# First input chunk loaded by column halves, first weights loaded whole, and one set of down forms moved by three units, in a one-core gated attention and MLP kernel

## The chip, the core and the metric

The kernel runs on one core of a Trainium2 chip. The core has a matrix engine (PE), a vector engine (DVE), a scalar engine (ACT), GpSimd (POOL) and a queue engine (SP); each takes its own instructions strictly in order and waits on semaphores for the others. PE writes to eight PSUM banks of 128 partitions x 2 KB, from which DVE or ACT copy results to SBUF. DMAs are issued from the queues of SP, ACT and POOL and all run on the same 16 DMA engines. The metric is device time in microseconds (us), the median of several executions; lower is better.

## What is computed

```python
def reference(A_x, A_wqkv, A_wo, B_x, B_w_gate, B_w_up, B_w_down, gate_w):
    x = A_x                                           # 1 x 2048 x 1024, bf16
    g = _sigmoid((x * gate_w).sum(-1, keepdims=True))
    a = _A_ref(x, A_wqkv, A_wo)   # 32 heads of 32, each position sees 8 positions, 2 apart
    b = _B_ref(x, B_w_gate, B_w_up, B_w_down)         # gelu(x Wg) * (x Wu), then Wd; 3584 wide
    return g * a + (1 - g) * b
```

## The kernel before

All large products are done with seven instead of eight block products (a Strassen scheme of Winograd's form). A *unit* is one 2x2 block product: 256 output rows of one projection against one half ("super chunk") of 1024 rows of the input. In it PE does seven forms of four matmuls of 128x128 by 128x512 each: `p1` (L11 R11), `p2` (L12 R21), `p5` (S1 T1), `p6` (S2 T2), `p73` (S3 T3 and S4 R22) and `p4` (L22 T4). R11 to R22 are quarters of the transposed input, T1 to T4 differences of them; L11, L12, L22 are quarters of the weights, S1 to S4 sums of them. Sums and differences are made on DVE ahead of their use: `sums_pair` (four `TENSOR_TENSOR` of 128x1024 at L313) for a pair of gate and up weights, and for the first input T1 to T4 by `T` in `head` (L1260). ACT copies most results out of PSUM (L349 to L397); each `p73` ends in one DVE add, L389, which frees two banks that the next units need.

The order on each engine is written out by hand. `head` does the first two weight pairs (four units, `f[0]` to `f[3]`) while the input is still arriving. The input's first two 512-row chunks come as loaded rows (`load_xn`), are transposed on PE in 128x128 blocks (`pe_transpose_chunk`, L217, four blocks into one bank as a *group*) and copied from PSUM by DVE (L223) and ACT (L221) in turn. In `head` the order is: transposes of chunk 0; `p1` of f[0] and f[1]; `patterns` (a small PE transpose L262, then DVE copies L264, L265); `p2` of f[0] and f[1]; f[2] and f[3]'s first forms; transposes of chunk 1; T1; then the weight sums of both pairs (`s0`, `s1`) spread between the other differences; the gate's matmuls (`gate_chunk`, L272); and `p5` of all four, `p6`, `p73`, `p4`. The weights of the two pairs arrive by `load_pair` (L168) in column halves of 128, so that L11 and L12 of both are there first, then the input's second chunk, then the other column halves, which only the sums and `p4` read. All these loads go through SP's queue, except two of the first chunk's four on ACT's.

After `head` a loop runs units 2 to n-1. Between two units' forms DVE runs background tasks, picked by priority and by a credit of planned DVE time per unit (`run_bg`). Among them: products of the local attention (L581, L588), their reduction on PE with `R_` (L593, 24 small matmuls in a row), softmax (L688 to L710), and `t_forms`, which makes differences of the down and output weights for the last stage, in nine sets of two blocks (L869 once, L872 twice, for a set), and stores them to DRAM. Sets 4 and 5 (`N1` and `N1 + 1`) are loaded together at unit `TB` and may be formed from unit `TB + 1` on.

Of the kernel before, what the change touches and what calls it, by code (L numbers as in the profile page):

```python
# [10 lines left out]
BF16 = mybir.dt.bfloat16  # L11
# [4 lines left out]
P = 128  # L16
SC = 512
# [5 lines left out]
NJ = 4  # L23
SJ = AC // NJ
NEG = -1.0e9
NWARM = 6
QG = 4

KB = 512
# [34 lines left out]
def _win_ap(src: bass.AP, dims):  # L64
    return AP(src.tensor, src.offset, [list(src.ap[0])] + [list(d) for d in dims])
# [3 lines left out]
def kernel(  # L69
# [12 lines left out]
    nc = tc.nc  # L82
# [3 lines left out]
    x = A_x.rearrange("b s d -> (b s) d")  # L86
    o2 = out.rearrange("b s d -> (b s) d")
    KT = D // P
    HK = KT // 2
# [13 lines left out]
    def reg(kb, n):  # L103
        o = int(kb * KB)
        return arena[:, o:o + n]

    def reg3(kb, a, b):
        return reg(kb, a * b).rearrange("p (a b) -> p a b", a=a)

    def reg4(kb, a, b, c):  # L110
        return reg(kb, a * b * c).rearrange("p (a b c) -> p a b c", a=a, b=b)

    def regf(kb, n):
        return reg(kb, 2 * n).bitcast(F32)
# [3 lines left out]
    def bank(i):  # L118
        return banks[:, i, :]
# [18 lines left out]
    with tc.manual_schedule(engines={mybir.EngineType.PE, mybir.EngineType.DVE, mybir.EngineType.Activation,  # L138
                                    mybir.EngineType.SP, mybir.EngineType.Pool}):
        xn = [reg3(R_XN + 8 * i, 4, D) for i in range(2)]  # L140

        def load_xn(c):
            for j in range(4):
                (nc.scalar if c == 0 and j % 2 else nc.sync).dma_start(
                    out=xn[c % 2][:, j, :], in_=x[c * SC + j * P:c * SC + (j + 1) * P, :])

        load_xn(0)
        warm = reg(R_ST, SC)
        V.memset(warm, 0.0)
        for i in range(NWARM):  # L150
            pw = bank((2, 4, 6, 0)[i % 4])
# [8 lines left out]
        raw0 = reg4(R_W0, 2, KT, 2 * P)  # L160
        raw1 = reg4(R_W0 + 8, 2, KT, 2 * P)
        sums0, sums1 = (reg(o, 4 * 2 * HK * P).rearrange("p (f m k n) -> p f m k n", f=4, m=2, k=HK)
                        for o in (R_WQK + 48, R_W0 + 16))

        def load_pair(dst, i, a=0, b=2 * P, k0=0, k1=KT):
            c0 = 2 * P * i
            for m, src in ((0, B_w_gate), (1, B_w_up)):
                nc.sync.dma_start(out=dst[:, m, k0:k1, a:b],  # L168
                                  in_=src[k0 * P:k1 * P, c0 + a:c0 + b].rearrange("(k p) n -> p k n", p=P))

        gwr = small.tile([KT, P], BF16, tag="gwr", bufs=1)
        nc.gpsimd.dma_start(out=gwr[:], in_=gate_w.rearrange("(k p) -> k p", p=P))
        load_pair(raw0, 0, 0, P, 0, HK)
        load_pair(raw0, 0, 0, P, HK, KT)
        load_pair(raw1, 1, 0, P)
        load_xn(1)
        load_pair(raw0, 0, P, 2 * P)
        load_pair(raw1, 1, P, 2 * P)

        class XF:  # L180
            pass
# [2 lines left out]
        for s in range(2):  # L184
            b0 = R_X[s]
            f = XF()
# [10 lines left out]
        def flat(a):  # L197
            return a.rearrange("p a b -> p (a b)")
# [8 lines left out]
            f = xf[s]  # L207
            TT(out=flat(f.T3), in0=flat(f.R22), in1=flat(f.R12), op=ALU.subtract)

        def pe_transpose_chunk(c, dst, slots, by_k=False):  # L210
            order = [(j, k0) for j in range(4) for k0 in range(0, KT, 4)]
            if by_k:
                order.sort(key=lambda g: g[1])
            for n_, (j, k0) in enumerate(order):
                p_ = bank(slots[n_ % len(slots)]).bitcast(BF16)[:, 0:SC].rearrange("p (a b) -> p a b", a=4)
                for kk in range(4):
                    nc.tensor.transpose(out=p_[:, kk, :], in_=xn[c % 2][:, j, (k0 + kk) * P:(k0 + kk + 1) * P],  # L217
                                        identity=ident[:])
                d = dst[:, k0:k0 + 4, j * P:(j + 1) * P]
                if n_ % 2 == 1:  # L220
                    nc.scalar.copy(out=d, in_=p_)  # L221
                else:
                    V.tensor_copy(out=d, in_=p_)  # L223
# [34 lines left out]
        def patterns():  # L258
            with nc.allow_low_precision("block pattern of zeros and ones"):
                V.tensor_reduce(out=R_[:], in_=ident[:].rearrange("p (h d) -> p h d", d=4), axis=AX.X, op=ALU.add)  # L260
            pgw = bank(7).bitcast(BF16)[:, 0:KT]
            nc.tensor.transpose(out=pgw, in_=gwr[:], identity=ident[0:KT, 0:KT])  # L262
            gwc = small.tile([P, KT], BF16, tag="gwc", bufs=1)
            V.tensor_copy(out=gwc[:], in_=pgw)  # L264
            V.tensor_copy(out=gwrep, in_=gwc[:].rearrange("p (k o) -> p k o", o=1).to_broadcast([P, KT, GC]))  # L265
# [61 lines left out]
        for c in range(2, 4):  # L327
            dst = (xf[1].c1, xf[1].c2)[c - 2]
# [73 lines left out]
        now = [0]  # L402
# [69 lines left out]
        def at_end(n, fn):  # L472
            post.setdefault(n, []).append(fn)
# [321 lines left out]
        for s in range(2):  # L795
            for t in range(NT):
                n_ = Q0 + NT * s + t
# [44 lines left out]
        N1 = 4  # L842
        TB = Q0 + 2 * NT + 1
        TC = NQKV + 1

        def tf_set(q):
            o = R_TF[q % 3] if q < N1 or q >= N1 + 2 else R_TB[q - N1]
            return [reg3(o + NP * k, NP, SC) for k in range(4)]

        def tf_load(q):  # L850
            i0 = NP * q
            for k, a in enumerate(((0, 0), (0, 1), (1, 0), (1, 1))):
                for sl, src in r_parts(*a, i0, i0 + NP):
                    nc.sync.dma_start(out=tf_set(q)[k][:, sl.start - i0:sl.stop - i0, :], in_=src)

        tf_q = [0]

        def t_forms():
            for q in range(NQ):
                tf_q[0] = q  # L860
                if q in (N1 + 1, N1 + 2):
                    tft.prio = 3.9 if q == N1 + 1 else 4.5
                    tasks.sort(key=lambda t_: t_.prio)
                while q >= N1 and now[0] < (TB if q < N1 + 2 else TC) + 1:
                    yield None
                r11, r12, r21, r22 = tf_set(q)
                n_ = NP * SC
                both = _win_ap(flat(r11), [[n_, 2], [1, n_]])
                TT(out=both, in0=_win_ap(flat(r12), [[2 * n_, 2], [1, n_]]), in1=both, op=ALU.subtract)  # L869
                yield 1.14  # L870
                for o_, a, b_ in ((r22, r22, r11), (r21, r21, r22)):
                    TT(out=flat(o_), in0=flat(a), in1=flat(b_), op=ALU.subtract)  # L872
                    yield 0.61
                for k, t in enumerate((r11, r22, r12, r21)):
                    nc.gpsimd.dma_start(out=t_d[k][:, NP * q:NP * q + NP, :], in_=t)
                if q + 3 < (N1 if q < N1 else NQ if q >= N1 + 2 else 0):
                    tf_load(q + 3)
# [5 lines left out]
        tft = bg(t_forms(), 6, Q0 + 4)  # L883

        def tf_close():
# [3 lines left out]
            tasks.sort(key=lambda t_: t_.prio)  # L889
            load_v()  # L890

        at_end(TFE - 1, tf_close)

        plan = [dict(A11=4, R11=5, A12=2, R21=7, A21=6, A22=3, T1=1, T2=9, S=8, AD=0, L5=4, R5=5, L6=7, R6=1,
                     T3=8, L7=4, R7=5, T4=9, L4=1, R4=7, R22=6),
# [333 lines left out]
        n = len(units)  # L1229
# [19 lines left out]
        def head():  # L1249
            xs, f = xf[0], []  # L1250
            for w, sm, o in ((raw0, sums0, R_ATTN), (raw1, sums1, R_PROD)):
                for m in range(2):
                    u = Unit(gu_forms(w, sm, m), xs, ("gate", "up")[m], None)
                    u.T = reg3(o + 4 * m, 2, SUP)
                    f.append(u)
            units[0:Q0] = f[2:]
            for u, x, v, y, z in zip(f, (3, 5, 1, 7), (1, 7, 3, 5), (0, 2, 4, 6), (1, 3, 5, 7)):
                u.lie(x, v, y, z)
            f[3].fin = lambda: bg(h_task(f[2].T, f[3].T, 1, 0), 0, now[0] + 1)
            T = lambda o_, a, b_: TT(out=flat(o_), in0=flat(a), in1=flat(b_), op=ALU.subtract)  # L1260
            s0, s1 = sums_pair(raw0, sums0), sums_pair(raw1, sums1)

            pe_transpose_chunk(0, xs.c1, (3, 5, 1, 7))
            f[0].p1_()
            f[1].p1_()
            patterns()
            f[0].p2()
            f[1].p2()
            f[2].p1_()
            f[3].p1_()  # L1270
            f[2].p2()
            pe_transpose_chunk(1, xs.c2, (3, 5, 1), True)
            T(xs.T1, xs.R12, xs.R11)
            next(s0)
            next(s1)
            f[3].p2()
            for c in range(2):
                gate_chunk(c, bank(3 + 2 * c))
            next(s0)
            T(xs.T2, xs.R22, xs.T1)  # L1280
            next(s1)
            T(xs.T3, xs.R22, xs.R12)
            for i, u in enumerate(f):
                u.p5(regf(R_XN + 2 * i, SC))
            for g in (s0, s0, s1, s1):
                next(g)
            T(xs.T4, xs.R21, xs.T2)
            for u in f:
                u.p6()
            next(sq0)  # L1290
            next(sq0)
            for u in f[:3]:
                u.p73()
            for g in (sq0, sq0, sq1, sq1):
                next(g)
            for u in f[:3]:
                u.p4()
            bg(h_task(f[0].T, f[1].T, 0, 0), 0, Q0 + 1)
# [59 lines left out]
```

## Time and profile before

| | |
|---|---|
| median of 3 executions | 718.57 us (717.97 to 718.95) |
| the profiled execution | 718.77 us |
| its span, first to last instruction | 717.0 us |
| granted TensorE clock, mean of the core | 1.000 |
| PE idle before matmuls, waiting for L389 on DVE | 2.2 us in 2 waits |
| input and weights: packets of 256 bytes, 14 to 16 us | 217 GB/s |
| input and weights: packets of 2 KB, 19 to 21 us | 388 GB/s |
| a later moment with weight rows of 512 bytes, 296 to 297 us | 352 GB/s |

In the timelines a line gives start, busy time (both in us), engine, source line, operation, what it writes and reads with shapes, and a count; in brackets stands how long the engine had been idle before and what ended that. The chain of waits is followed back from the last instruction to whatever released each step, so what stands in it set the end of the run.

### The profile page before, as it was taken

Reading aid. Unit: us, or ns where it says so; the run is one execution under the profiler, and the core shown is the slowest. Engines: PE = TensorE matmul, PEld = TensorE weight load, DVE = VectorE, ACT = ScalarE, POOL = GpSimd, SP = SyncE. Lnnn points to the kernel's source line nnn. Section 1 sums busy time; section 2 is a strip of 40 time slices with the busy share of each in tenths; the row PEclk is TensorE's granted clock in tenths of the full one; section 3 lists DMA queues with packets and bytes.
Section 4 is the critical chain, followed back from the end, with each engine's and each line's share of the span. In section 5 each row is a group of like instructions: output and inputs, shape, how many; then the busy total and the mean of one; then the engine's idle time right before and its main releaser. Section 6 shows DMA issues by size and latency. Waiting matters only on the chain.

```text
span 717.0 us, 10673 instructions
## 1 busy us (share of the span) xinstructions
PE 705.7 (98%) x4043; PEld 408.4 (57%) x4099; DVE 669.0 (93%) x633; ACT 330.7 (46%) x603; POOL 142.4 (20%) x245
## 2 busy tenths in 40 slices
PE   8999999999999999999999999999999999999998
PEld 5466666655544444444444444444447886758887
DVE  3969989989999999999999999999699899799997
ACT  5554445444466565555555555555322321132431
POOL 1223445323232332121300010101100002100011
PEclk9999999999999999999999999999999999999999
DMA  9975434478285667765762763474950799995951
GB/s 252 274 188 169 151 125 154 155 239 306 92 269 175 214 216 240 223 214 180 234 178 89 279 208 122 161 262 148 426 226 29 300 405 397 417 431 218 403 211 59
DMA packets 94707, 162.03 MB, mean 226 GB/s; under 512 B 23632, under 2 KB 71152, under 8 KB 90304
## 3 DMA queue, kind: packets, MB, share of 16 engines
q1 hardware_dynamic: 77632, 105.46, 42.7%
q0 software_dynamic: 16304, 48.29, 19.9%
q10 hardware_dynamic: 720, 7.60, 2.7%
q8 instruction: 32, 0.52, 0.3%
q14 instruction: 19, 0.16, 0.1%
HBM read 112.17 MB, written 54.14 MB: 232 GB/s over the span
## 4 chain that ended last, share of the span: by engine, by line
PE 91%; DVE 3%; DMA 3%; issue 1%; ACT 0%; DVEq 0%; POOLq 0%; ACTq 0%
PE banks L343 63%; PE banks L1046 19%; PE banks L1079 7%; PE banks L593 2%; DMA arena<-h_d 1%; DMA h_d<-arena 1%; DVE arena L389 1%; DVE arena L753 1%; PE banks L217 1%; DVE arena L747 1%; DMA arena<-in_A_x_dram 0%; DVE arena L313 0%; DVE arena L588 0%; DVE arena L1260 0%; DVE arena L581 0%
## 5 line engine op out<-in xcount | busy, mean ns | idle before, releaser
L343 PE MATMUL banks<-arena 128*128 128x512 bf16 x2191 | 484.1, 379 | 5.4 <-DVE arena L389 2.2
L343 PEld LDWEIGHTS <-arena 128*128 128x128 bf16 x2240 | 245.9, 110 | 242.2 <-issue 8.1
L1046 PE MATMUL banks<-arena 128*128 128x256 bf16 x1260 | 138.5, 273 | 0.0
L1046 PEld LDWEIGHTS <-arena 128*128 128x128 bf16 x1260 | 123.3, 98 | 15.4 <-issue 0.5
L389 DVE TENSOR_TENSOR arena<-banks,arena 128x1024 bf16<-128x1024 f32 x80 | 97.4, 1219 | 11.1 <-PE banks L343 6.5
L370 ACT COPY arena<-banks 128x512 f32<-128x512 f32 x80 | 46.9, 587 | 129.7 <-PE banks L343 129.7
L351 ACT CAST arena<-banks 128x512 bf16<-128x512 f32 x104 | 60.9, 585 | 42.8 <-PE banks L343 42.2
L747 DVE TENSOR_TENSOR arena<-arena 128x4096 bf16<-128x4096 bf16 (+1 forms) x41 | 73.5, 1818 | 0.3
L753 DVE TENSOR_TENSOR arena<-arena 128x2048 bf16<-128x2048 bf16 (+2 forms) x54 | 68.1, 1261 | 0.9
L250 POOL DMA_DIRECT2D h_d<-arena x28 | 20.4, 731 | 222.6 <-DVE arena L244 144.6
L1079 PE MATMUL banks<-arena 128*128 128x512 bf16 x281 | 62.6, 379 | 0.7 <-DMA arena<-h_d 0.4
L378 ACT COPY banks<-banks 128x512 f32<-128x512 f32 x80 | 45.6, 570 | 23.7 <-PE banks L343 20.8
L1004 DVE TENSOR_TENSOR arena<-arena 128x2304 bf16<-128x2304 bf16 x40 | 53.3, 1352 | 0.5
L365 ACT COPY banks<-banks 128x512 f32<-128x512 f32 x80 | 46.1, 576 | 14.2 <-PE banks L343 13.1
L1051 ACT COPY banks<-banks 128x256 f32<-128x256 f32 x60 | 21.4, 356 | 62.2 <-PE banks L1046 62.0
L588 DVE TENSOR_TENSOR arena<-arena 128x4096 bf16<-128x4096 bf16 x21 | 47.9, 2284 | 0.3 <-ACT arena L370 0.2
L1079 PEld LDWEIGHTS <-arena 128*128 128x128 bf16 x288 | 28.1, 98 | 34.2 <-DMA arena<-h_d 0.9
L349 ACT ACTIVATE arena<-banks 128x512 bf16<-128x512 f32 x56 | 33.5, 597 | 20.4 <-PE banks L343 20.4
L927 DVE TENSOR_TENSOR arena<-arena 128x2048 bf16<-128x2048 bf16 (+1 forms) x40 | 41.7, 1111 | 0.0
L313 DVE TENSOR_TENSOR arena<-arena 128x1024 bf16<-128x1024 bf16 x64 | 41.1, 685 | 0.5
L1012 DVE TENSOR_TENSOR arena<-arena 128x2304 bf16<-128x2304 bf16 x28 | 37.7, 1352 | 0.2
L244 DVE TENSOR_TENSOR arena<-arena 128x2048 bf16<-128x2048 bf16 x28 | 34.0, 1216 | 2.8 <-ACT arena L351 2.8
(92 smaller groups left out, 448.2 us busy)
## 6 DMA issues: line engine op xcount, KB each, us to landing
arena<-t_d SPq DMA_DIRECT2D x8, 2304.0 KB, 9.6
h_d<-arena POOLq DMA_DIRECT2D x28, 512.0 KB, 4.4
arena<-w_c SPq DMA_DIRECT2D x12, 1152.0 KB, 13.2
t_d<-arena POOLq DMA_DIRECT2D x36, 256.0 KB, 5.4
arena<-h_d SPq DMA_DIRECT2D x6, 1536.0 KB, 12.1
arena<-in_B_w_down_dram SPq DMA_DIRECT2D x28, 256.0 KB, 6.6
arena<-in_B_w_gate_dram SPq DMA_DIRECT2D x14, 512.0 KB, 5.4
arena<-in_B_w_up_dram SPq DMA_DIRECT2D x14, 512.0 KB, 4.2
```

The lines of the kernel that those rows point to most:

```text
L343: self.pe = nc.tensor.matmul(ps, lhsT=self.L[form](kt), rhs=rhs[:, kt, :], start=(start and kt == 0), stop=(kt == HK - 1), skip_group_chec ...
L351: nc.scalar.copy(out=o_, in_=i_)
L365: nc.scalar.copy(out=self.Y, in_=self.X)
L370: nc.scalar.copy(out=self.p5s, in_=self.V)
L378: nc.scalar.copy(out=self.Z, in_=self.Y)
L389: TT(out=self.T[:, :, c2s], in0=pair, in1=self.p5s.rearrange("p (o n) -> p o n", o=1).to_broadcast([P, 2, SC]), op=ALU.add)
L588: TT(out=dst, in0=_win_ap(q, [[sq, 2], [0, NWIN], [1, AC]]), in1=_win_ap(k, [[sk, 2], [-DIL, NWIN], [1, AC]]), op=ALU.mult)
L747: TT(out=prod2[:, t % 4:t % 4 + m, :], in0=flat(ab).rearrange("p (o n) -> p o n", o=1).to_broadcast([P, m, NWIN * AC]), in1=_win_ap(v[:, t ...
L753: TT(out=h(0) if w > 1 else o_[:, t:t + m, :], in0=h(0), in1=h(1), op=ALU.add)
L1004: TT(out=o_, in0=a, in1=b_, op=op)
L1046: nc.tensor.matmul(c(i, h, j), lhsT=l[:, kt, j * P:(j + 1) * P], rhs=r[:, kt, :], start=False, stop=(kt == KH - 1), skip_group_check=True)
L1079: nc.tensor.matmul(ps, lhsT=L[:, i, j * P:(j + 1) * P], rhs=R[:, i, :], start=(start and q == 0), stop=(q == NK - 1), skip_group_check=not ...
```

## The change

The first chunk is loaded in column halves: two DMAs of 256 rows x 512 columns (one on SP's, one on ACT's queue), then the row halves of the first pair's weights at full width (gate on SP, up on ACT), then the other column halves of the input, then the rest of the first pair, the whole second pair, and the second chunk as two DMAs. Transposes of chunk 0 are split into the blocks of the first four column blocks, `p1` of f[0] and f[1], and the blocks of the last four. Each group now goes to half a bank given by a list. Chunk 1's transposes use eight half banks in place of three banks and come after `p2` of f[3]; all weight sums are placed ahead of them on DVE, `patterns` after `p2` of f[0], and the second chunk's differences after them. There is one more warm-up matmul. Set 5 of `t_forms` may be formed from unit `TB + 4` on, where it is also forced to be done by that unit's end.

```diff
-NWARM = 6
+NWARM = 7
...
-        def load_xn(c):
-            for j in range(4):
-                (nc.scalar if c == 0 and j % 2 else nc.sync).dma_start(
-                    out=xn[c % 2][:, j, :], in_=x[c * SC + j * P:c * SC + (j + 1) * P, :])
-
-        load_xn(0)
+        def load_xn(c, k0, k1, eng):
+            cs = slice(k0 * P, k1 * P)
+            for i in range(2):
+                r0 = c * SC + 2 * i * P
+                eng[i].dma_start(out=xn[c % 2][:, 2 * i:2 * i + 2, cs],
+                                 in_=x[r0:r0 + 2 * P, cs].rearrange("(j p) d -> p j d", p=P))
+
+        both_q = (nc.sync, nc.scalar)
+        load_xn(0, 0, HK, both_q)
...
-        def load_pair(dst, i, a=0, b=2 * P, k0=0, k1=KT):
+        def load_pair(dst, i, k0=0, k1=KT, eng=(nc.sync, nc.sync)):
             c0 = 2 * P * i
             for m, src in ((0, B_w_gate), (1, B_w_up)):
-                nc.sync.dma_start(out=dst[:, m, k0:k1, a:b],
-                                  in_=src[k0 * P:k1 * P, c0 + a:c0 + b].rearrange("(k p) n -> p k n", p=P))
+                eng[m].dma_start(out=dst[:, m, k0:k1, :],
+                                 in_=src[k0 * P:k1 * P, c0:c0 + 2 * P].rearrange("(k p) n -> p k n", p=P))
...
-        load_pair(raw0, 0, 0, P, 0, HK)
-        load_pair(raw0, 0, 0, P, HK, KT)
-        load_pair(raw1, 1, 0, P)
-        load_xn(1)
-        load_pair(raw0, 0, P, 2 * P)
-        load_pair(raw1, 1, P, 2 * P)
+        load_pair(raw0, 0, 0, HK, both_q)
+        load_xn(0, HK, KT, both_q)
+        load_pair(raw0, 0, HK, KT)
+        load_pair(raw1, 1)
+        load_xn(1, 0, KT, (nc.sync, nc.sync))
...
-        def pe_transpose_chunk(c, dst, slots, by_k=False):
-            order = [(j, k0) for j in range(4) for k0 in range(0, KT, 4)]
-            if by_k:
-                order.sort(key=lambda g: g[1])
-            for n_, (j, k0) in enumerate(order):
-                p_ = bank(slots[n_ % len(slots)]).bitcast(BF16)[:, 0:SC].rearrange("p (a b) -> p a b", a=4)
+        def pe_transpose_chunk(c, dst, slots, ks):
+            for n_, (k0, j) in enumerate((k0, j) for k0 in ks for j in range(4)):
+                b, h = slots[n_]
+                p_ = bank(b).bitcast(BF16)[:, h * SC:(h + 1) * SC].rearrange("p (a b) -> p a b", a=4)
...
-                while q >= N1 and now[0] < (TB if q < N1 + 2 else TC) + 1:
+                while q >= N1 and now[0] < (TB + 3 * (q - N1) if q < N1 + 2 else TC) + 1:
                     yield None
...
+        def tf_close_b():
+            while tf_q[0] < N1 + 2:
+                tft.step()
+
         at_end(TFE - 1, tf_close)
+        at_end(TB + 4, tf_close_b)
...
-            pe_transpose_chunk(0, xs.c1, (3, 5, 1, 7))
+            pe_transpose_chunk(0, xs.c1, [(i, 0) for i in (3, 5, 1, 7)], (0,))
             f[0].p1_()
             f[1].p1_()
+            pe_transpose_chunk(0, xs.c1, [(i, h) for h in range(2) for i in (1, 7)], (HK,))
+            f[0].p2()
             patterns()
-            f[0].p2()
             f[1].p2()
+            for _ in range(4):
+                next(s0)
             f[2].p1_()
             f[3].p1_()
+            for _ in range(4):
+                next(s1)
             f[2].p2()
-            pe_transpose_chunk(1, xs.c2, (3, 5, 1), True)
+            f[3].p2()
+            pe_transpose_chunk(1, xs.c2, [(i, h) for i in (3, 5, 1, 7) for h in range(2)], (0, HK))
             T(xs.T1, xs.R12, xs.R11)
-            next(s0)
-            next(s1)
-            f[3].p2()
             for c in range(2):
                 gate_chunk(c, bank(3 + 2 * c))
-            next(s0)
             T(xs.T2, xs.R22, xs.T1)
-            next(s1)
             T(xs.T3, xs.R22, xs.R12)
             for i, u in enumerate(f):
                 u.p5(regf(R_XN + 2 * i, SC))
-            for g in (s0, s0, s1, s1):
-                next(g)
             T(xs.T4, xs.R21, xs.T2)
```

## The prediction

> **What bounds the kernel now.** The page's first part comes first: PE is busy for nearly the whole span.
>
> ```profile
> PE 705.7 (98%) x4043; PEld 408.4 (57%) x4099; DVE 669.0 (93%) x633; ACT 330.7 (46%) x603; POOL 142.4 (20%) x245
> ```
>
> PE is idle for 717.0 - 705.7 = 11.3 us in all, so an edit that leaves the number of matmuls alone can win a few us at most, but can lose any amount: wherever PE is made to wait, the end moves. The chain of waits in order of time shows where that happens in the head (start, us, what):
>
> ```profile
> 4.12 2.90 PE banks L217 x28
> ...
> 7.05 0.43 DVE arena L223
> ...
> 7.53 1.89 PE banks L343 x8
> ...
> 16.75 1.22 DVE arena L1260
> 17.96 0.61 DVE arena L313
> ...
> 18.62 6.65 PE banks L343 x30
> ```
>
> PE goes through transposes, waits for the last copy, starts `p1` of f[0] at 7.53, and meets one more DVE stretch (T1 and one weight sum) before `p5` of f[0] at 18.62. From there PE never stops until 173. So the first part of the change is priced by one question: when does this `p5` start? The timeline gives the durations, and one line how the sums are placed now, behind the start of `p5`:
>
> ```profile
> 5.62 0.42 DVE L223 COPY arena<-banks 128x512 bf16<-128x512 bf16 x1 [0.43 <-PE banks L217]
> 6.05 0.59 ACT L221 COPY arena<-banks 128x512 bf16<-128x512 bf16 x1 [0.27 <-PE banks L217]
> 9.56 0.16 DVE L264 COPY gwc<-banks 128x8 bf16<-128x8 bf16 x1 [1.89 <-PE banks L262]
> 9.76 0.29 DVE L265 COPY arena<-gwc 128x256 bf16<-128x256 bf16 x1
> 14.28 0.42 DVE L223 COPY arena<-banks 128x512 bf16<-128x512 bf16 x1 [4.23 <-PE banks L217]
> 22.56 2.49 DVE L313 TENSOR_TENSOR arena<-arena 128x1024 bf16<-128x1024 bf16 x4
> ```
>
> The waits of PE name two later stops, of 1.44 and 0.75 us, both for L389. The timeline around the first:
>
> ```profile
> 159.22 1.22 DVE L869 TENSOR_TENSOR arena<-arena 128x2048 bf16<-128x2048 bf16 x1 [0.55 <-DMA arena<-in_B_w_down_dram]
> 162.82 1.23 DVE L869 TENSOR_TENSOR arena<-arena 128x2048 bf16<-128x2048 bf16 x1 [0.92 <-DMA arena<-in_B_w_down_dram]
> 163.76 1.48 PE L593 MATMUL banks<-arena,ones_r 128*32 128x512 bf16 x24
> 166.55 1.75 DVE L688 TENSOR_REDUCE md<-banks 128x192 f32<-128x1536 f32 x1
> 173.34 1.22 DVE L389 TENSOR_TENSOR arena<-banks,arena 128x1024 bf16<-128x1024 f32 x1
> 174.61 10.74 PE L343 MATMUL banks<-arena 128*128 128x512 bf16 x48 [1.44 <-DVE arena L389]
> 179.19 1.22 DVE L389 TENSOR_TENSOR arena<-banks,arena 128x1024 bf16<-128x1024 f32 x1
> 184.87 1.22 DVE L389 TENSOR_TENSOR arena<-banks,arena 128x1024 bf16<-128x1024 f32 x1
> ```
>
> The two L869 begin sets 4 and 5. Set 5 costs DVE its wait and work and makes everything behind it late, up to the L389 at 173.34.
>
> **The head, step by step.** I walk the built program's order, with what each instruction waits for, using these durations. A handover from PE to a copy takes about 0.2 us (last transpose of a group at 4.55, copy at 4.77), from a copy to PE 0.05.
>
> *First half.* The first 512 KB of input now must land whole; before, the first two DMAs (the same bytes) landed by about 4.2. Seven warm-up matmuls at 0.43 end at 1.20 + 3.0 = 4.2, so the added one costs at most that wait. I start transposes at 4.35 (bounds 4.2 to 4.9: packets of 1 KB have no row here). Sixteen at 107 ns take 1.7; the last copy is ACT's 0.59. `p1` starts at 6.9, 0.6 before 7.53. ACT's two added DMA issues (0.45 each) lie in its idle 2.02 us ahead of 5.19.
>
> *Second half.* Eight `p1` matmuls end at about 8.8. The next groups use both halves of banks 1 and 7, and the built order makes the third group wait for DVE's copy of the first and the fourth for ACT's copy of the second, although the halves differ. ACT also has f[1]'s copy in front. So `p2` of f[0] starts at about 11.1. Its quarter is R21, needed whole: a second stop that the old order did not have.
>
> *Sums.* `patterns` now sits behind this `p2` (0.87). L264 starts at 12.2, the first sum at 12.2 + 0.16 + 0.29 = 12.65, and eight sums at 2.49 / 4 = 0.62 end at 17.6. On DVE all eight stand ahead of chunk 1's copies. Before, most of them lay behind `p5`'s start, covered by PE.
>
> *Chunk 1.* PE has finished `p2` of f[3] by 11.1 + 0.87 + 0.17 + 20 x 0.216 = 16.5 and transposes one group; the second half of each bank waits for DVE's copy of the first. DVE is free at 17.6. One round is copy 0.42, handover 0.05, eight transposes about 0.45, handover 0.19: 1.11. Three rounds and the fourth copy end at 17.6 + 3.3 + 0.4 = 21.3, T1 takes 1.22, and ACT's last copy and the gate's last matmuls end at about the same time. `p5` starts at 22.8 against 18.62: **+4.2 us**. A round may be as short as 0.84 (DVE's copies at 14.28 and 15.12 stood so far apart), which gives +3.4; a late input or a late clock gives up to +6.5.
>
> *Loads.* Weights in rows of 512 bytes have no row in the head. Bounds: 217 GB/s (rows of 256 bytes) and 388 GB/s (2 KB), nearest 320 to 350 in later moments with weight rows of that width; I take 300 while queues mix. The 4.2 MB up to chunk 1's end then land at about 15.4 (13.4 to 18.4). They are wanted at 16.5, and behind the sums only at 17.6, so the load order is covered, or costs up to 1 us. SP issues nine DMAs instead of sixteen ahead of the query and key weights, so what queues there (those weights, the DMA transposes) comes no later. The forms taken from behind `p5` win nothing, since PE did not wait there.
>
> *The clock.* Full clock is granted from 6.58 us (transposes go from 107 ns to about half that), and PE had run almost only transposes since 4.12. I keep 6.58. [...]
>
> **The set of down forms.** Removing set 5 lets L688 follow the end of L593 (163.76 + 1.41 + 0.2 = 165.4) instead of 166.55. The chain from there to L389 took 173.34 - 166.55 = 6.79, so it starts at 172.2, ends at 173.4, and PE, ready at 173.17, waits 0.25 instead of 1.44: -1.15. Then the set comes back. L389's next partner follows 5.85 later (178.05); behind it now stand set 5's 1.22 + 1.42 - 0.06 = 2.58, then the next softmax's 5.68 to the following L389: it starts at 178.05 + 2.58 + 5.68 = 186.3 and ends at 187.5. PE needs it two units after the first, 173.4 + 56 x 0.216 = 185.5: a new wait of **2.0**, and about 0.5 at the next L389, since a moved product (1.14) lies there. Queued behind the set are that softmax and every L389; PE waits for these. Its four POOL stores move too, and POOL is 20% busy. Further on, credits pair DVE's steps differently; the two orders walked to the end differ by -0.2 to +0.9, I take +0.3. Sum -1.15 + 2.0 + 0.5 + 0.3 = **+1.7** (bounds -1.2 and +3).
>
> **Sum.** 4.2 + 1.7 = +5.9 on the profiled execution, 718.77 (717.0 of span and 1.8 around it): 724.7. That execution lies 0.2 above the median, so I predict **724.5**.
>
> **Rivals.**
> 1. *The moved set fits into idle DVE time.* Only the -1.15 is left: 718.57 + 4.2 - 1.15 = 721.6. For it: DVE has idle microseconds elsewhere. Against: from 166.55 to 184.87 no idle time stands in DVE's timeline, and the new place is inside it.
> 2. *The clock comes later.* With two further stops in the head, PE may miss the period that counts; then eight matmuls (0.21 each) and 16 transposes (0.05) run at half speed: +2.5, 727.0. For: PE stands still at 6.1 to 6.9. Against: it stood still at 7.24 to 7.53 too. [...]
> 3. *The loads decide.* Second chunk after 17.6, at the 217 GB/s end: +1, 725.5, or +2 with the queues mixing, 726.5.
> 4. *Not slower: PE alone sets the head.* If copies never hold PE, its work up to `p5` is seven warm-ups 3.0, 16 transposes at 107 ns and 48 at 56 (4.4), 32 matmuls 6.9, 0.17 and the gate's 1.05: 15.5, so `p5` at 1.2 + 15.5 = 16.7, a gain of 1.9, and with +1.7 later 718.4; without the later loss 715.5. It decides once `p5` starts before 18.62 - 1.7 = 16.9. For: half banks double the slots. Against: the built waits tie both halves of a bank, and 5 us of sums stand ahead of the copies.
> 5. *Nothing measurable*, parts cancelling: 718.6.
>
> **How the numbers follow.** Forecast 0.66, rival 1 0.12, rival 2 0.09, rival 3 0.06, rival 4 0.05, rival 5 0.02. What the measurement can tell from no change is about 0.2%, 1.4 us. Slower: the forecast and rivals 1 to 3, 0.93; rival 4 gives 0.04 to faster and 0.01 to same; with rival 5 same is 0.03. The range takes rival 1 at its low end and reaches past rivals 2 and 3 at its high end: 721.5 to 727.3.
>
> **What would show it.** Right: `p1` near 6.9, a second stop ahead of f[0]'s `p2` near 11, eight L313 in a row on DVE to 17.6, four spaced L223 behind them, `p5` near 22.8; PE's wait of 1.44 shrunk and a new one near 2 us, two units later. Wrong: `p5` before 20; DVE idle ahead of chunk 1's copies (then loads decide); granted full clock later than 7; no wait over 1 us behind the moved set.

## The result, and the profile after

| | before | after |
|---|---|---|
| median, both measured side by side | 718.5 us (717.56 to 718.95, 6) | 724.98 us (724.07 to 726.4, 6) |
| the profiled execution | 718.77 us | 724.22 us |
| its span | 717.0 us | 722.4 us |
| `p5` of f[0] starts | 18.62 us | 22.54 us |
| PE waits for L389, sum | 2.2 us in 2 | 3.0 us in 6 |

The ratio is 1.0094 with a 95% interval of 1.0079 to 1.0109: the change makes the kernel slower by 0.8 to 1.1%. The changed kernel's times lie in two groups, 724.07 to 724.22 and 725.73 to 726.4, and the profile shows one of the lower group; what the upper one is comes under the clock. The page's engine line is almost the old one:

```profile
PE 706.7 (98%) x4044; PEld 407.9 (56%) x4100; DVE 669.5 (93%) x639; ACT 330.8 (46%) x603; POOL 142.3 (20%) x245
```

PE has 1.0 us more of work, of which the seventh warm-up is 0.43, and 722.4 - 706.7 = 15.7 us of idle time in place of 11.3. The loss is waits. PE's timeline in the head shows them (start, busy us, what, and in brackets the idle time before):

```profile
6.29 1.89 PE L343 MATMUL banks<-arena 128*128 128x512 bf16 x8 [0.71 <-ACT arena L221]
...
10.39 1.02 PE L343 MATMUL banks<-arena 128*128 128x512 bf16 x3 [0.68 <-ACT arena L221]
...
17.58 0.61 PE L217 MATMUL banks<-ident,arena 128*128 128x128 bf16 x8 [1.20 <-DVE arena L223]
18.77 0.61 PE L217 MATMUL banks<-ident,arena 128*128 128x128 bf16 x8 [0.58 <-DVE arena L223]
...
21.15 0.38 PE L217 MATMUL banks<-ident,arena 128*128 128x128 bf16 x4 [0.58 <-DVE arena L223]
...
22.54 7.73 PE L343 MATMUL banks<-arena 128*128 128x512 bf16 x34
```

`p1` of f[0] starts 1.24 us earlier than before. Then comes the second stop ahead of `p2`, and the four rounds in which PE waits for a DVE copy of the lower half of a bank before it may write the upper half. DVE's side of the same stretch:

```profile
12.04 5.15 DVE L313 TENSOR_TENSOR arena<-arena 128x1024 bf16<-128x1024 bf16 x8
17.11 0.42 DVE L223 COPY arena<-banks 128x512 bf16<-128x512 bf16 x1
18.30 0.42 DVE L223 COPY arena<-banks 128x512 bf16<-128x512 bf16 x1 [0.77 <-PE banks L217]
```

Eight sums stand in a row ahead of the first copy of chunk 1. After that DVE itself is idle for 0.77 us in every round of 1.19, and PE for 0.58: the two take turns, and each stands still while the other works. Later, around the moved set of forms, PE and DVE show:

```profile
178.03 12.25 PE L343 MATMUL banks<-arena 128*128 128x512 bf16 x55 [0.20 <-DVE arena L389]
192.12 6.20 PE L343 MATMUL banks<-arena 128*128 128x512 bf16 x27 [1.85 <-DVE arena L389]
198.59 6.63 PE L343 MATMUL banks<-arena 128*128 128x512 bf16 x30 [0.26 <-DVE arena L389]
```

```profile
182.61 1.22 DVE L389 TENSOR_TENSOR arena<-banks,arena 128x1024 bf16<-128x1024 f32 x1
183.75 1.22 DVE L869 TENSOR_TENSOR arena<-arena 128x2048 bf16<-128x2048 bf16 x1
185.00 1.42 DVE L872 TENSOR_TENSOR arena<-arena 128x1024 bf16<-128x1024 bf16 x2
186.33 2.83 DVE L705 TENSOR_REDUCE md<-arena 128x192 f32<-128x1536 f32 x1
...
190.85 1.22 DVE L389 TENSOR_TENSOR arena<-banks,arena 128x1024 bf16<-128x1024 f32 x1
```

Set 5 (L869, L872) now stands between one L389 and the softmax step L705, and the next L389 can begin only at 190.85; the matmuls at 192.12 wait 1.85 us for it.

How late the changed kernel runs against the old one, read off where the same work starts in both timelines: 3.92 us at `p5`, 4.2 at 62 us, 4.7 at 165 us, 5.9 at 209 us (the set has added 1.2), 6.2 at 518 us. Before, PE waited 0.36 us for a DMA at 527 us; coming later it does not wait there. 5.7 are left at 550, and 5.5 at the end of the span.

### The profile page after: what moved, and what is told of

It is laid out like the page before. It is cut to its first block, busy times and chain, and to the rows that moved or that the text cites. A ratio compares the mean times of both kernels' runs of the same rounds, so it can differ in the third digit from the quotient of the medians.

```text
span 722.4 us, 10678 instructions
## 1 busy us (share of the span) xinstructions
PE 706.7 (98%) x4044; PEld 407.9 (56%) x4100; DVE 669.5 (93%) x639; ACT 330.8 (46%) x603; POOL 142.3 (20%) x245
## 5 line engine op out<-in xcount | busy, mean ns | idle before, releaser
L389 DVE TENSOR_TENSOR arena<-banks,arena 128x1024 bf16<-128x1024 f32 x80 | 97.5, 1219 | 16.7 <-PE banks L343 7.4
L747 DVE TENSOR_TENSOR arena<-arena 128x2048 bf16<-128x2048 bf16 (+1 forms) x44 | 73.8, 1705 | 0.3
L250 POOL DMA_DIRECT2D h_d<-arena x28 | 20.4, 731 | 217.9 <-DVE arena L244 141.1
L932 DVE TENSOR_TENSOR arena<-arena 128x2048 bf16<-128x2048 bf16 (+1 forms) x40 | 41.7, 1112 | 0.0
```

The lines of the kernel that those rows point to most:

```text
L389: TT(out=self.T[:, :, c2s], in0=pair, in1=self.p5s.rearrange("p (o n) -> p o n", o=1).to_broadcast([P, 2, SC]), op=ALU.add)
L747: TT(out=prod2[:, t % 4:t % 4 + m, :], in0=flat(ab).rearrange("p (o n) -> p o n", o=1).to_broadcast([P, m, NWIN * AC]), in1=_win_ap(v[:, t ...
```

## Experiments

Each time is a median over several executions, and the ratio is to the kernel before, measured beside it. `p5` is where `p5` of f[0] starts in the profile; before it was 18.62. When the clock rises to full differs from execution to execution, so where that was late in the profile, the cell says it.

| what | us (range) | ratio to before (95%) | `p5` |
|---|---|---|---|
| e1 forms only | 719.51 (719.08 to 720.19) | 1.0021 (1.0012 to 1.0030) | 18.34 |
| e2 head only | 723.15 (722.89 to 724.07) | 1.0073 (1.0060 to 1.0085) | 24.91, full clock from 10.6 |
| e3 head, banks in turn | 720.46 (719.47 to 722.12) | 1.0031 (1.0021 to 1.0040) | 19.83 |
| e4 head, sums back | 722.45 (721.58 to 723.50) | 1.0065 (1.0052 to 1.0079) | 22.49 |
| e5 forms one unit earlier | 719.0 (718.01 to 721.4) | 1.0008 (0.9997 to 1.0020) | 20.21, full clock from 9.8 |
| e6 loads only | 720.7 (719.95 to 721.57) | 1.0029 (1.0018 to 1.0040) | 19.94, full clock from 9.1 |
| e7 head with most stops taken out | 718.56 (717.76 to 720.2) | 0.9999 (0.9988 to 1.0011) | 19.84, full clock from 10.6 |
| e8 after, six warm-ups | 726.28 (725.32 to 726.38) | 1.0102 (1.0085 to 1.0119) | 24.46 |
| e9 before, seven warm-ups | 718.32 (717.80 to 718.87) | 1.0003 (0.9994 to 1.0012) | 18.48 |
| e10 after again | 726.26 (725.44 to 726.58) | 1.0111 (1.0097 to 1.0125) | 24.5 |
| e11 after with two repairs | 722.52 (720.62 to 722.77) | 1.0055 (1.0041 to 1.0069) | 20.46 |
| e12 loads only, SP held up | 718.82 (718.39 to 719.88) | 0.9999 (0.9989 to 1.0008) | 19.70 |

### Which part costs

e1 makes the change of the forms alone in the kernel before; e2 is the changed kernel with this part taken back:

```diff
-                while q >= N1 and now[0] < (TB if q < N1 + 2 else TC) + 1:
+                while q >= N1 and now[0] < (TB + 3 * (q - N1) if q < N1 + 2 else TC) + 1:
...
+        at_end(TB + 4, tf_close_b)
```

> The kernel before, with only set 5 of the down forms moved to unit TB + 4. Theory (the set returns in front of the next softmax): PE's wait for L389 near 174 us shrinks from 1.44 to about 0.2, a new one of about 1.9 us stands two units later and one of about 0.3 behind it; +1.2 us on the kernel before, about 719.7 us. Rival (the set finds idle DVE time): the 1.44 us wait goes and nothing comes back, about 717.3 us.

> The changed kernel with set 5 back at unit TB + 1. Theory (the head costs what it costs whatever the set does): p5 of f[0] at 22.5 us as in the changed kernel, about +4.3 us on the span of the kernel before, about 1.2 us less than the changed kernel, and the two L389 waits of the kernel before (1.44 and 0.75 us) back. Rival (the two parts interact): less than 3 or more than 6 us on the kernel before.

Against 718.1 for the kernel before, e1 loses 1.4 us and e2 5.05; together 6.45, and the whole change lost 6.48. So close an agreement is partly luck, since the changed kernel's median lies between its two groups. The profiles say it more directly: from 165 to 209 us the moved set makes PE 1.18 us later in the changed kernel, and 1.18 us in e1. In e1 the waits come out as in the changed kernel, 0.20, then this one, then 0.26:

```profile
187.18 6.21 PE L343 MATMUL banks<-arena 128*128 128x512 bf16 x28 [1.84 <-DVE arena L389]
```

e2 lost more than the 4.3 expected. Its profile starts with work that takes twice as long as elsewhere:

```profile
6.93 3.57 PE L343 MATMUL banks<-arena 128*128 128x512 bf16 x8 [0.68 <-ACT arena L221]
```

The same eight matmuls took 1.89 us in the profiles of before and after: here full clock came only at 10.6 us. `p5` starts at 24.91 in place of 22.54, 2.4 us later. This explains the profile, at 724.07 the slowest of the five executions; when full clock came in the others is not known. The two later waits for L389 came back as 1.21 and 0.53 us, where 1.44 and 0.75 were expected.

### The head: tied banks or sums

e3 takes e2 and gives chunk 1's groups their half banks in another order; e4 takes e2 and puts the sums back behind T1, with the banks as changed:

```diff
-            pe_transpose_chunk(1, xs.c2, [(i, h) for i in (3, 5, 1, 7) for h in range(2)], (0, HK))
+            pe_transpose_chunk(1, xs.c2, [(i, h) for h in range(2) for i in (3, 5, 1, 7)], (0, HK))
```

> As the head alone, but chunk 1's eight groups take the four banks in turn (3, 5, 1, 7, then their other halves) instead of both halves of one bank after another. Theory A (the two halves of a bank are tied, so PE and DVE take turns): the four waits of 0.6 to 1.2 us in the transposes shrink to one of about 0.5, p5 at about 20.3, 2.2 us less than the head alone. Theory B (the sums ahead of the copies are the cost): DVE still comes to the copies at 17.1 only, p5 stays above 21.8.

> As the head alone, but the weight sums on DVE go back to where the kernel before had them, behind T1; the banks stay tied. Theory A (tied banks): the copies begin at about 16.4 instead of 17.1, the rounds of about 1.19 us stay, then T1 and the first sum: p5 at about 22.2, at most 0.5 us less than the head alone. Theory B (the sums are the cost): p5 at 19 to 20, 2.5 us less or more.

PE's timeline of e3:

```profile
13.62 2.76 PE L343 MATMUL banks<-arena 128*128 128x512 bf16 x12 [0.48 <-DMA arena<-in_B_w_up_dram]
16.22 2.27 PE L217 MATMUL banks<-ident,arena 128*128 128x128 bf16 x32
...
19.83 10.52 PE L343 MATMUL banks<-arena 128*128 128x512 bf16 x47 [0.27 <-DVE arena L1260]
```

All 32 transposes of chunk 1 run in one piece, with all eight sums still ahead of the copies, and `p5` starts 2.7 us earlier than in the changed kernel (0.2 of it was there at `p1` already). So the rounds were the cost. In e4 the rounds stay (transposes at 16.95, 18.14, 19.33 and 20.52, each after 0.58 us of idle PE), and the sums, moved back, end up ahead of `p5` once more:

```profile
22.49 7.72 PE L343 MATMUL banks<-arena 128*128 128x512 bf16 x35 [0.51 <-DVE arena L313]
```

That is 0.05 us better than 22.54, so with tied banks the place of the sums hardly counts. (The medians of e4 and e2 differ by 0.7, a little more than theory A allowed; their ranges overlap.) The first line of e3 shows what the stops had covered: PE waits for the up weights of the second pair, which now load whole. This wait also gave DVE time for the sums. In e11 below, where PE is not held there, the sums last until 17.6 us and PE waits 0.58 for the first copy behind them: with the banks untied, the sums are not free.

e7 asks what the column halves could bring at best. The weights load by column halves as before, only two sums stand ahead of `p5`, `p1` of f[2] and f[3] fills the second stop, and no group goes to a bank whose copy is still to come:

```diff
+            pe_transpose_chunk(0, xs.c1, [(7, 0), (6, 0), (4, 0)], (HK,), range(3), "V")
+            f[2].p1_()
+            pe_transpose_chunk(0, xs.c1, [(6, 1)], (HK,), (3,), "V")
+            f[3].p1_()
...
+            pe_transpose_chunk(1, xs.c2, [(i, 0) for i in (3, 5, 1, 3)], (0,))
```

> The changed head with its three suspected costs taken out, and the set of forms back in its old place: each group of transposes goes to a bank whose copy is not waited for, p1 of f[2] and f[3] stand between the groups of the second half, weights load by column halves as before, and only two sums stand ahead of p5. Theory (PE is nearly always busy in the head, so the column halves themselves are worth only what the stops of before summed to, about 1.4 us, and the later first landing takes part of that back): no stop over 0.6 us up to 18, the fifth unit starts 0.2 to 0.5 us earlier than before, time 717.6 to 718.4. Rival (the column halves are worth the 1.2 us by which p1 comes earlier): time 716.9 to 717.3.

One stop of 0.67 us stays, ahead of `p1` of f[0], a little over the 0.6 that the theory allowed. The result, 718.56, is a little above the theory's 717.6 to 718.4 and cannot be told from before. The rival is refuted, as a gain of 1.2 us lies outside the interval: an earlier `p1` is worth nothing by itself. A likely reason, not tested apart, is that PE has the same work ahead of `p5` and was idle there for about a microsecond. The profile fell into an execution with late full clock, so where its fifth unit starts says nothing.

### The set of forms: the place or the set

> The kernel before with one edit: the second set of down forms (set 5) begins two units after the first instead of three, so it does not stand right ahead of the next softmax. Theory (the loss of the moved set is its place: it stood ahead of a softmax whose result PE needs two units later): the new wait of 1.8 us near 187 is gone, the first wait is between 0.2 and 0.6, and the time is within 0.6 us of before, 717.6 to 718.7. Rival (a set of forms costs about 1.2 us of DVE time wherever it is put between these softmaxes): a stop of over 1 us stays, or some stops that add up to it, further on, and the time is 719.3 to 720.

The edit is `TB + 2 * (q - N1)` in e1's place of `3`. PE's timeline has one wait of 0.20, and where e1 had 1.84 there is none for 157 matmuls:

```profile
175.58 34.86 PE L343 MATMUL banks<-arena 128*128 128x512 bf16 x157 [0.20 <-DVE arena L389]
```

So the wait belongs to the place ahead of the softmax. A stop of 0.89 at 511 us is new. The median is 0.3 above the range that the theory gave and 0.3 below the rival's; the interval of the ratio, from -0.2 to +1.4 us, includes no change. The set in this place shows no measurable cost, and no gain.

### The loads, and what they do 40 us later

e6 is the kernel before with the weights of the first two pairs loaded whole ahead of the second chunk:

```diff
-        load_pair(raw0, 0, 0, P, 0, HK)
-        load_pair(raw0, 0, 0, P, HK, KT)
-        load_pair(raw1, 1, 0, P)
-        load_xn(1)
-        load_pair(raw0, 0, P, 2 * P)
-        load_pair(raw1, 1, P, 2 * P)
+        load_pair(raw0, 0, k0=0, k1=HK)
+        load_pair(raw0, 0, k0=HK, k1=KT)
+        load_pair(raw1, 1)
+        load_xn(1)
```

> The kernel before with one edit: the weights of the first two pairs load whole ahead of the second chunk of x; the first chunk and every order of PE, ACT and DVE stay. Theory (the loads are covered in the changed kernel only because its other stops are longer): the second chunk lands at about 16.0 instead of 13.4 and the up weights of the second pair at about 13.4, PE waits for DMA in the head, p5 of f[0] starts 1.4 to 1.8 us later than 18.62 and the time is 719.5 to 720.0. Rival (the loads are covered by themselves): p5 within 0.4 us of 18.62, time 717.8 to 718.5.

It costs 0.18 to 0.40%, more than either theory gave, and not in the way expected. `p5` at 19.94 comes near the theory's 20.0 to 20.4 by accident: in the profile the first rows of x came 0.5 us later than before and full clock at 9.1 in place of 6.6 us, and PE shows no wait for the second chunk. But PE stops for 0.96 us at 59.06 and 0.44 at 87, which before it did not. What is late there? First DVE, SP and POOL before, then the same three in e6 (lines of e6 are two lower than those of before, so L579 is L581):

```profile
52.96 1.23 DVE L581 TENSOR_TENSOR arena<-arena 128x2048 bf16<-128x2048 bf16 x1 [1.17 <-DMA h_d<-arena]
```

```profile
46.41 9.04 SPq L854 DMA_DIRECT2D arena<-in_B_w_down_dram  x12
```

```profile
45.66 1.50 POOL L250 DMA_DIRECT2D h_d<-arena  x2
```

```profile
56.65 1.22 DVE L579 TENSOR_TENSOR arena<-arena 128x2048 bf16<-128x2048 bf16 x1 [2.71 <-DMA h_d<-arena]
```

```profile
43.99 8.56 SPq L852 DMA_DIRECT2D arena<-in_B_w_down_dram  x12
```

```profile
46.97 1.49 POOL L248 DMA_DIRECT2D h_d<-arena  x2
```

In the kernel before, SP issues the twelve loads of down weights from 46.41 on, behind POOL's two stores of h_d (products of gate and up units, to DRAM) at 45.66. With four DMAs fewer in its queue (twelve in place of sixteen; the expectations for e12 miscount them as six), SP gets through its DMA transposes earlier and issues the down weights from 43.99, three microseconds *ahead* of the stores. The DMA view (KB each, median us from issue to landing) shows the stores of before, e6 and e12 in this stretch:

```profile
h_d<-arena POOLq DMA_DIRECT2D x2, 512.0 KB, 5.2
```

```profile
h_d<-arena POOLq DMA_DIRECT2D x2, 512.0 KB, 8.1
```

```profile
h_d<-arena POOLq DMA_DIRECT2D x2, 512.0 KB, 4.3
```

In these profiles the landing goes with the order of issue on the two queues: 5.2 us with the loads issued 0.75 us behind the stores, 8.1 with the loads 2.98 us ahead of them, and 4.3 with the loads 3.25 us behind (e12: stores at 46.74, loads from 49.99).

The stores can lose this race from the other side too, without any change of the loads. In e5 a late clock put `p5` at 20.21; POOL issued the stores at 47.25, 0.5 us behind the down weights at 46.72, they took 6.9 us, DVE waited 2.54 us for them, and PE stopped for 0.44 at 86.68. So e6's stop of 0.44 is no mark of the load order, and as e6's own stores came 1.3 us later than before, behind its late head, its profile alone does not say how much of the wait the load order made. e12 does.

e12 keeps e6's loads and puts seven tiny loads, whose data nothing uses, into SP's queue, so that SP is late again:

```diff
+        late = small.tile([1, 7 * 4], BF16, tag="late", bufs=1)
+        for i in range(7):
+            nc.sync.dma_start(out=late[:, i * 4:(i + 1) * 4], in_=x[0:1, i * 4:(i + 1) * 4])
         for c in range(2, 4):
             dst = (xf[1].c1, xf[1].c2)[c - 2]
```

> The kernel with the load order alone (weights whole ahead of the second chunk), and in addition seven loads of 8 bytes, which nothing reads, in SP's queue ahead of its DMA transposes; so SP comes to these, and to the down weights behind them, as late as before the change. Theory (the load order costs because SP, with six DMAs fewer to issue, starts the down weights 2.4 us earlier and they get ahead of the two stores of h_d on POOL, for whose landing DVE and then PE wait): the down weights start at 46 us or later, the stores of h_d land within 6.5 us of their issue instead of 8.1, DVE's wait for them falls from 2.7 to under 1.8 us, PE's stop of 0.96 us near 59 falls under 0.4, and the time is 718.6 to 719.9. Rival (the loads cost by the later landing of the second chunk and of the second pair's weights in the head): stop and stores may change, the time stays 720.3 to 721.2.

They hold SP up by more than was meant: the down weights start at 49.99. The stores land after 4.3 us, DVE does not wait for them at all, PE's stop near 59 is gone, and the ratio holds no change. In the head this execution shows the price of the load order itself: PE waits 0.72 us for the up weights of the second pair, and `p5` comes 1.08 late. The end of the profile does not show it, since PE's later stops shrink: 0.57 us in place of 1.44 at 175, 0.52 in place of 0.75 at 280, none at 527. There DVE or a DMA came last, and PE, coming later, waits less.

The rival, that the loads cost by their landing in the head, is refuted for the larger part of e6's loss. A smaller part may be left: nine of the 17 executions of the kernel before beside e12 took 719.25 us or more, and against the other eight e12's median is 0.7 higher. The first rows of x, which neither kernel touches, landed between 4.1 and 4.8 us in these executions, so a few tenths at `p5` mean nothing.

### The clock and the warm-up

e10 is the changed kernel unaltered, e8 the same with `NWARM = 6`, e9 the kernel before with `NWARM = 7`.

> The changed kernel once more, for the spread of its times. [...] Rival (the spread is of DMA landings): the upper group shows full clock from under 7 us on and a later landing.

> The changed kernel with six warm-up matmuls instead of seven. Theory (the added warm-up ends ahead of the first landing and costs nothing; when full clock is granted varies from execution to execution whatever the warm-ups): the same times in two groups, about 724.1 and about 726, median 724 to 726.4. Rival (the seventh warm-up, by filling the gap before the first transposes, decides whether full clock comes early): the granted clock comes at 6.5 us or later in the profile and all times are near 726.

> The kernel before with one edit: seven warm-up matmuls instead of six. Theory (the seventh ends at about the first landing and costs nothing; it fills the stop of PE ahead of the first transposes): median 717.8 to 718.4, first transposes no later than 4.4. Rival 1 (it holds up the transposes by 0.2 to 0.3 us, which PE never makes good): 718.3 to 718.6. Rival 2 (six leave a gap of over a microsecond, which in some executions costs the early grant of full clock; seven close it): executions above 720 are gone, and the mean of the times falls by 0.3 or more.

All of e10's executions are in the upper group. PE's windows of its profile (stretch, its length, PE's busy time, matmuls, granted clock, DMA share, GB/s):

```profile
16.00:18.00 2.00, 0.77 (x7) 1.00 1.05 387
18.00:20.00 2.00, 1.24 (x16) 0.95 1.05 386
20.00:22.00 2.00, 1.03 (x9) 0.50 1.05 387
...
26.00:28.00 2.00, 2.00 (x10) 0.84 1.69 96
```

Between 16.39, where the transposes of chunk 1 begin, and 19.8 PE is idle for 1.41 and 0.58 us, in the waits of the rounds, and the clock is halved from 19.8 to 26.6 us. `p5`, at 22.54 in the first profile, starts at 24.5 at half speed, 2.0 us later. Of these, 0.6 were there at `p1` already (full clock from 6.15 in place of 4.75); the rest is the halved clock, which goes on past `p5`. At the end the two profiles are 2.3 us apart, about the distance of the groups. Of the rival's two marks one is there, full clock under 7 us, though it did not last; the other is not, as the first transposes start at 4.33 in both profiles. A mean granted clock under 0.999 was measured only in kernels with the rounds: 0.995 to 0.998 in three of six executions of the changed kernel, two of five of e2, three of five of e4, four of five of e8 and all four of e10, against 0.999 or 1.000 in every execution of the kernel before and of the other versions. By these figures the halved clock is a cost of the tied banks on top of the rounds themselves.

In e8 the same happened at 19.7, and its times lie in e10's group (also the 726.32 of the execution whose mean clock is 1.000), so that six or seven warm-ups make no difference that these runs show; theory and rival had each half of it wrong, since only the upper group appeared, and full clock first came at 6.05. e9 agrees with its theory: ratio 1.0003, first transposes at 4.30. (Its 718.32 lies in rival 1's range as well; but the profile's `p5` is 0.14 earlier than before, not later.) Whether a seventh warm-up makes a late first grant rarer stays open: beside e9 no execution of the kernel before was above 719.01 either, though beside e5 to e8 and beside e12 5 of 29 and 6 of 17 were above 720.1. It does not rule one out: e2 and e7 have seven warm-ups, and full clock came at 10.6 us.

### The change repaired

> The changed kernel with two edits: the groups of chunk 1 take the four banks in turn, so that the two halves of one bank are four groups apart, and the moved set begins one unit earlier. Theory (the loss is made of tied banks, 2.7 us, the place of the moved set, about 0.9 us, and of what the column halves and the load order cost, which stays): the four spaced copies and the wait of 1.85 us are gone, time 720.2 to 721.2. Rival (the two losses are not additive, since DVE that is no longer held in the head is then held elsewhere): 721.8 to 723.

The edits are those of e3 and e5, both in the changed kernel. The wait of 1.85 is gone, and of the rounds' stops one of 0.58 is left, at 17.98. But the time is mostly above the theory's range and in the rival's. The rival is right that DVE is then held elsewhere; where, neither had said. PE's timeline shows e6's stop again:

```profile
59.69 4.48 PE L343 MATMUL banks<-arena 128*128 128x512 bf16 x20 [1.08 <-DVE arena L389]
```

DVE had waited 2.61 us for the stores of h_d. In the changed kernel, with `p5` 2 us later than here, PE did not stop at this place. No version tried beats the kernel before.

## Why the prediction was right, and where it was not

The mechanisms were those of the prediction: tied halves of a bank, sums in a row on DVE, a set of forms ahead of a softmax. The forecast, 724.5, lies between the two groups; +5.9 was forecast for the profiled execution, and 724.22 - 718.77 = +5.45 measured. By stages these are 3.92 at `p5` (4.2 forecast), 0.75 more up to 165 us (nothing forecast), 1.18 for the moved set (1.35) and -0.4 behind it (+0.3). That the misses of the parts cancel in part is luck. So is how near 724.98 is to 724.5: three executions lie in each group, and e10's four, all in the upper one, gave 726.26.

- *First half, second stop, sums.* `p1` at 6.29 (said 6.9), `p2` at 10.39 (11.1), the last sum's end at 17.2 (17.6), for the reasons given. The 0.6 is the clock: the sum took full clock from 6.58, the profile had it from 4.75, and where it came at 6.15 or later `p1` starts at 6.89 and 6.93 (e10, e2).
- *Chunk 1.* Rounds of 1.19 (1.11), `p5` +3.92 (+4.2; the terms as listed add up to 22.6, not 22.8, with 22.54 measured). e3 shows that the tied halves are worth 2.5 to 2.7 us of it. The prediction gave the eight sums ahead of the copies weight as well; e4 shows that with tied banks it hardly matters where they stand. With the banks untied they were hidden in e3 by a wait for weights, and cost PE a stop of 0.58 in e11.
- *The set of forms.* 0.20, 1.85 and 0.26 for the predicted 0.25, 2.0 and 0.5. By e1's median the part costs 1.4 (said 1.7), by the profiles 1.18 up to 209 us. Rival 1, that the set fits into idle time, fell with the wait of 1.85. e5 shows that one unit earlier this wait goes, but the gain of 1.15 that rival 1 counted on does not appear.
- *Loads.* "Covered" held: the second chunk landed at 16.04 (15.4 said) and PE shows no wait for DMA in the head. It was covered by the other stops; in e3, e4 and e12 PE waits 0.48, 0.20 and 0.72 us for the up weights. (The bounds of 13.4 and 18.4 do not follow from the rates named for them: 388 and 217 GB/s give about 12 and 21 us, counted as the 15.4 was.) The step that failed is the one on SP's queue, "what queues there comes no later". It came earlier, and that was the harm: the load order alone costs 2 us (e6), the load order with SP held up nothing that the ratio shows (e12). In the changed kernel most of this lay hidden behind the head's larger delay: DVE waits 0.60 us for the stores, and PE loses 0.75 in all between `p5` and 165 us. Rival 3 looked for the loads' cost only in the head.
- *Clock.* The profile of after had full clock from 4.75 us, but the sum's "I keep 6.58" names one case of several. Rival 2 gave +2.5 and 727.0 for a clock that is missing at the start. e2's profile is that case (+2.4 at `p5`). No run shows the "period that counts" which rival 2 names; the runs show a first full clock between 3.9 us (e1) and 10.6 (e2, e7). The upper group of the changed kernel has another form of it that the prediction did not name, the clock taken back in the rounds, at about the same price, 2.3 us with a first grant 1.4 us later; its times are 725.4 to 726.6.
- *Rival 4*, PE alone sets the head, fell. Even in e7, with most of the stops taken out, the new order brought nothing measurable.

## What to carry to other kernels

Half banks gave more slots here only where consecutive groups did not share a bank: with two groups in one bank after each other PE and the copying engine took turns, and each turn cost 0.58 us of PE with both engines partly idle (after, e2); with the banks in turn the 32 transposes ran in one piece (e3). Four DMAs taken out of SP's queue moved the twelve loads behind them forward by 2.4 us, past two stores on POOL's queue that they used to follow, and these landed after 8.1 us in place of 5.2 (e6); look for stores whose landing somebody waits for, even 40 us later. Stores that come later lose in the same way: 6.9 us in e5, where they came 0.5 us behind the loads. Work that the bounding engine starts earlier is a gain only as far as that engine was idle before: in e7 `p1` starts 0.7 us earlier, and its 718.56 cannot be told from before.

## What the runs showed of the hardware

When full clock first came differed between executions: at 3.9 us in e1, 4.75 in the first profile of after, 6.15 in e10, 6.58 in the kernel before, 10.6 in e2 and e7. The eight matmuls of `p1` took 3.57 us ahead of it in e2, and 1.89 behind it in the profiles of before and after. `p5` of e2, with 10.6, is 2.4 us later than in the changed kernel with 4.75 (24.91 and 22.54).

What the first grant depends on is not shown. e2 and e10 do the same work up to `p1`, at most 0.04 us apart: warm-ups from 1.20, 16 transposes from 4.37 and 4.33, a stop of 0.68 and 0.67, `p1` at 6.93 and 6.89. Full clock came at 10.6 in the one and at 6.15 in the other.

What in the rounds takes it back is not shown either. In e10 full clock went at 19.80 and returned at 26.63; from 16.39 to the loss PE had waited 1.41 and 0.58 us. The profile of e2 has the same waits in its rounds, ending at 19.95 and 21.14, and its granted clock is 1.00 there; in the first profile of after they are 1.20 and 0.58, and the clock stayed as well.
